# Turning the combined attention weights in 32-square pieces on VectorE and through DRAM, for chunks 3 to 11 of a sliding-window attention and feed-forward kernel

## The chip, the cores and the metric

The kernel runs on 1 core of one Trainium2 chip. The metric is the device time of one execution in microseconds (us). The kernel before takes 695.46 us (median of 3 runs, 695.16 to 696.05).

## The reference

Attention over 4 batches, 8 heads, 768 positions and head size 64, where a query sees only the 4 first keys (sinks) and the last 128 keys. The output, 3072 tokens by 512, goes through two matrix products with a leaky rectifier between them. All of it is float32.

```python
scores = scale * q @ k.T                     # per batch and head, 768 x 768
keep = (key < n_sink) | ((query - key >= 0) & (query - key < window))
a = softmax(where(keep, scores, -1e9))
x = (a @ v) laid out as (3072, 512)
h = x @ w_in                                 # (3072, 2048)
g = maximum(h, 0) + alpha * minimum(h, 0)
out = g @ w_out                              # (3072, 512)
```

## The kernel before, in words

**Tiling.** The 3072 tokens are cut into 12 chunks of 256 queries (`NCHUNK`), three to a batch. A chunk is two query tiles of 128 (`u` is 0 or 1). For a head of a chunk there are three blocks of 128 keys and the 4 sinks. The heads are taken in four pairs (`p` is 0 to 3, `j` the head within its pair).

**Attention of a chunk** (`attention(c)`, in steps). Head by head: `prep_head` splits queries and keys of a loaded tile `stage` into high and low parts (L553 to L557); `unit` makes the scores by two matmuls into a bank `s` (L589, L590); `soften` adds the mask and takes the row's extreme on VectorE (L602), then the exponential on ScalarE (L606). `finish_head` takes the sums' reciprocals (L635, L636). Of a query tile's two key blocks, the older one is used only above the diagonal and the newer one only below and on it, so that both fit in one 128 by 128 square. L647 (L643 for the first tile of a batch) adds them, scaled, into the tile `comb`: 128 queries by 512, which holds four such squares, (head of the pair, query tile). `comb` tiles come from a ring of 4. After the eighth head `sink_step` prepares the sinks (L674, L675, L680, L683).

**Turning the weights.** The product with the values needs the weights with keys on the partitions. `trans(c, p)` does it for chunks 2 to 11: four TensorE transposes per pair, one per square, into one PSUM bank (L694), then two VectorE products of 512 elements each (L698) that read the bank, multiply by two triangles of ones (`tri`) and so part the older from the newer block again, into a tile `wa` (ring of 2). Chunks 0 and 1 (`SPLIT`) do this in another way and do not call it. From chunk 3 on (`PAIRED`) the steps at the end are: `trans` of pairs 0 and 1, `av_two(c, 0)`, `trans` of pairs 2 and 3, `av_two(c, 2)`. `av_two` multiplies two pairs with the sinks (L781) and the values (L711, in 24 or 16 short matmuls), and splits the result into `xh` and `xl` (L791, L792).

**Feed-forward of a chunk.** Sixteen slots `f`. `gemm1` (L806): 12 matmuls of 256 columns into one of two banks `h`; ScalarE and VectorE turn it into `gh` and `gl` (L810 to L813); `gemm2`, two slots later (`LAG`): six matmuls of 512 columns (L843, L844, L841). While chunk c is in its feed-forward, the steps of chunk c+1's attention are spread over its slots 1 to 12 (`SPAN`); slots 13 to 15 have none. The first `gemm1` of a chunk needs all of `xh` and `xl`.

**The order of the work** is computed by the class `Plan`. Each operation is recorded with its engine, a cost, and what it reads and writes. `draw` then runs a clock for each engine and picks, at each step, an operation that can begin soonest; among those of one engine that can begin within a short time it takes the one of lowest rank. The rank of a TensorE operation is its place in the program; any other operation has that of the first TensorE operation that needs it. A DMA issue on SP costs 0.45 us in the plan, and its data counts as landed 2 us, and the time for its bytes at 290 GB/s, after it begins. Every engine then gets its instructions in the planned order and works through them in that order, waiting where the planned time was wrong. Buffers of one ring (a "kind") are handed out strictly in the order in which the program asked for them:

```python
if len(f) <= n or not any(q[x] is v for x in range(min(len(q), n + 1))):
    ok = False
```

So a later `comb` tile can't be given out in the plan while an earlier request of that ring is still unserved. SP's queue carries the loads of `stage` (ring of 2, L436), the values (L451) and the stores of the output (L850).

Of the kernel before, what the change touches and what calls it, by code (L numbers as in the profile page):

```python
# [9 lines left out]
F32 = mybir.dt.float32  # L10
# [7 lines left out]
ALU = mybir.AluOpType  # L18

P = 128  # L20
# [23 lines left out]
PAIRED = 3  # L44
# [34 lines left out]
class Plan:  # L79
# [20 lines left out]
    def held(self, tile_):  # L100
        v = Value(None)
        v.at = tile_
        return v

    def op(self, engine, cost, run, reads=(), writes=(), tail=0.09, mode=None, nbytes=0, other=None, locks=False):
        o = Op(engine, cost, tail, run, self.rank if engine == "PE" else None)
        o.ways = {engine: (cost, run)}
        if other:
            o.ways[other[0]] = other[1:]
        o.born = self.rank  # L110
        if engine == "PE":
            self.rank += 1
        o.mode, o.nbytes, o.index = mode, nbytes, len(self.ops)
        seen = []
        for group, writing in ((reads, False), (writes, True)):
            for x in group:
                v, key = x if isinstance(x, tuple) else (x, None)
                if v not in seen:
                    seen.append(v)
                keys = [k for k in set(v.wrote) | set(v.read) if key is None or k is None or k == key]  # L120
                for k in keys:
                    o.before.update(v.wrote.get(k, ()))
                    if writing:
                        o.before.update(v.read.get(k, ()))
                if writing:
                    for k in keys:
                        if key is None or k == key:
                            v.wrote.pop(k, None)
                            v.read.pop(k, None)
                    v.wrote.setdefault(key, []).append(o)  # L130
                else:
                    v.read.setdefault(key, []).append(o)
        for v in seen:
            v.left += 1
        o.values = seen
        o.takes = [v for v in seen if v.kind]
        o.locks = locks
        self.ops.append(o)
        return o
# [144 lines left out]
def dve(n, fast=False):  # L284
    return 0.07 + (0.52e-3 if fast else 1.04e-3) * n


def cast(n, psum=False):
    return (0.045 if psum else 0.092) + 0.84e-3 * n
# [27 lines left out]
ISSUE = 0.45  # L317
# [3 lines left out]
def program(ctx, tc, qk, pairs, vp, vs, w, par, out):  # L321
    nc = tc.nc
# [4 lines left out]
    plan = Plan(tc)  # L327
    op, val, held = plan.op, plan.value, plan.held
# [5 lines left out]
    def several(name, n, shape, dtype):  # L334
        plan.kind(name, [pool.tile(shape, dtype, name=f"{name}{i}") for i in range(n)])

    several("stage", 2, [P, QC + KC], F32)
    several("kq", 2, [P, KC + 2 * QC], F32R)
    several("v", 2, [P, 3, 2, D], F32)
# [131 lines left out]
    def known(x):  # L471
        return V.setdefault(x, held(x))
# [38 lines left out]
    tri = pool.tile([P, 2, P], F32, name="tri")  # L511
# [27 lines left out]
    xh, xl, prep, comb, sink, ptile_, sums, rinv, nms, wt = {}, {}, {}, {}, {}, {}, {}, {}, {}, {}  # L539

    def bank(c, n, tag):
        return val("o" if c == 0 and n % 2 else tag)
# [67 lines left out]
    def finish_head(c, h):  # L610
        pt, nm, sm = ptile_.pop((c, h)), nms[c], sums[c]
        sk = sink[c]
        if h == H - 1:
            op("DVE", 0.1, lambda: nc.vector.tensor_tensor(fm, fm, nm.at.rearrange("p h u -> p (h u)"), ALU.max),
               reads=[nm], writes=[known("fm")])
        if c in SPLIT:
            op("POOL", 0.17, lambda: nc.gpsimd.tensor_copy(sk.at[:, :, h], pt.at[:, :, P:P + NS]), reads=[pt], writes=[(sk, h)])
            tp = bank(c, h, "pa")
            for u in range(2):
                o = 2 * u * P  # L620
                both = u > 0 or c % CPB > 0

                def turn(u=u, o=o, both=both):
                    if both:
                        nc.tensor.transpose(tp.at[:, o:o + P], pt.at[:, u, 0:P], ident)
                    nc.tensor.transpose(tp.at[:, o + P:o + 2 * P], pt.at[:, u, P + NS:], ident)
                op("PE", (1 + both) * TURN, turn, reads=[(pt, u), known("ident")], writes=[tp], tail=T_TAIL)
            t = val("comb")
            o = P if c % CPB == 0 else 0
            op("ACT", cast(4 * P - o, True), lambda: nc.scalar.copy(t.at[:, o:], tp.at[:, o:]), reads=[tp], writes=[t],  # L630
               other=("DVE", dve(4 * P - o), lambda: nc.vector.tensor_copy(t.at[:, o:], tp.at[:, o:])) if c == 0 else None)
            wt.setdefault((c, h // 2), []).append(t)
            return
        ri = val("ri")
        op("DVE", 0.15, lambda: nc.vector.tensor_scalar(ri.at[:, :2], sm.at[:, h], 1e-9, None, op0=ALU.add), reads=[(sm, (h, 0)), (sm, (h, 1))], writes=[ri])  # L635
        op("DVE", 0.08, lambda: nc.vector.reciprocal(ri.at[:, :2], ri.at[:, :2]), writes=[ri])  # L636
        if h % 2 == 0:
            comb[c, h // 2] = val("comb")
        cb = comb[c, h // 2]
        view = lambda: cb.at.rearrange("p (j u x) -> p j u x", j=2, u=2)[:, h % 2]  # L640
        for u in range(2):
            if u == 0 and c % CPB == 0:
                op("DVE", 0.2, lambda: nc.vector.tensor_scalar(view()[:, 0], pt.at[:, 0, P + NS:], ri.at[:, 0:1], None, op0=ALU.mult),  # L643
                   reads=[(pt, 0), ri], writes=[(cb, (h % 2, 0))])
                continue
            jk = val("jk")
            op("DVE", 0.28, lambda u=u, jk=jk: nc.vector.tensor_tensor_reduce(  # L647
                out=view()[:, u], in0=pt.at[:, u, 0:P], in1=pt.at[:, u, P + NS:], scale=ri.at[:, u:u + 1], scalar=0.0,
                op0=ALU.add, op1=ALU.max, accum_out=jk.at[:, u:u + 1]),
                reads=[(pt, u), ri], writes=[(cb, (h % 2, u)), jk])  # L650
        op("POOL", 0.2, lambda: nc.gpsimd.tensor_tensor(
            sk.at[:, :, h], pt.at[:, :, P:P + NS], ri.at[:, :2].unsqueeze(2).broadcast_to([P, 2, NS]), ALU.mult),
            reads=[pt, ri], writes=[(sk, h)])

    sinkT = {}

# [28 lines left out]
    def trans(c, p):  # L685
        if c in SPLIT:
            return
        tp, cb, tt = val("pa"), comb.pop((c, p)), val("wa")
        full = lambda: tt.at.bitcast(F32).rearrange("p (j u l x) -> p j u l x", j=2, u=2, l=2)

        def turn(j):
            for u in range(2):
                o = (2 * j + u) * P
                nc.tensor.transpose(tp.at[:, o:o + P], cb.at[:, o:o + P], ident)  # L694
        for j in range(2):
            op("PE", 2 * TURN, lambda j=j: turn(j), reads=[(cb, (j, 0)), (cb, (j, 1))], writes=[(tp, j)], tail=T_TAIL)
        for j in range(2):
            op("DVE", dve(4 * P), lambda j=j: nc.vector.tensor_tensor(  # L698
                full()[:, j], tp.at[:, j * QC:(j + 1) * QC].rearrange("p (u x) -> p u x", u=2).unsqueeze(2).broadcast_to([P, 2, 2, P]),
                tri.unsqueeze(1).broadcast_to([P, 2, 2, P]), ALU.mult), reads=[(tp, j), known("tri")], writes=[(tt, j)])  # L700
        wt[c, p] = tt

    def values(c, v, weights, a, stop=True):

        sets = [(1, slice(P, 3 * P), slice(0, 2 * P))]
        if c % CPB:
            sets.append((0, slice(0, P), slice(0, P)))
        sets.append((2, slice(3 * P, 4 * P), slice(P, 2 * P)))
        for n, (blk, ws, os) in enumerate(sets):
            for j in range(2):  # L710
                nc.tensor.matmul(a[j * D:(j + 1) * D, os], v[:, blk, j], weights(j)[:, ws], start=False, stop=stop and n == len(sets) - 1)  # L711
# [149 lines left out]
    def attention(c):  # L861
        def a_step(h, u):
            def run():
                if u == 0:
                    if h == 0 and c and c % CPB == 0:
                        vs_prep(c // CPB)
                    prep_head(c, h)
                    next_load()
                unit(c, h, u)
                if u == 1:  # L870
                    finish_head(c, h)
                    if h in (5, 6):
                        load_v(c, h - 5)
            return run
# [139 lines left out]
    with tc.If(bad != 0):  # L1014
# [3 lines left out]
        with tc.For_i(0, B, 1) as b:  # L1018
            for cc in range(CPB):
                x = general(nc, gen, ptile, cc, b, qk5, vp5, nsink, window, ident)  # L1020
# [162 lines left out]
```

## Time and profile before

| | |
|---|---|
| median of 3 runs | 695.46 us |
| the profiled execution: time, span | 695.24 us, 693.3 us |
| busy TensorE, VectorE, ScalarE, GpSimd | 680.6, 497.2, 408.2, 32.2 us |
| L694: TensorE transposes | 160, mean 273 ns from start to end |
| L698: VectorE products out of the bank | 80, mean 685 ns |
| DMA | 63.71 MB, 28155 packets |

The page of the profile gives busy times by engine, the span in 40 slices, the DMA queues, and the chain of work that ended last. Views of the trace give groups of instructions by line, stretches of time (windows), the chain in order of time, and the timeline of one engine. Matmuls overlap, so the mean time of one from start to end is longer than what it adds to the chain; VectorE's instructions overlap slightly too, so its "slot" is the distance from one start to the next.

### The profile page before, as it was taken

How to read it: one execution, taken by the hardware profiler on the slowest of the kernel's cores; microseconds unless marked ns; L12 is line 12 of the kernel's file. 1: busy time of each engine (PE TensorE's matmuls, PEld its weight loads, DVE VectorE, ACT ScalarE, POOL GpSimd, SP SyncE). 2: the span in 40 equal slices, each digit the busy share in tenths (PEclk: the TensorE clock that was granted, in tenths of full speed). 3: DMA queues.
4: the chain of work that ended last, by engine and by line, in shares of the span. 5: the costliest groups of instructions: out<-in, count | busy, mean ns of one | idle time of the engine just before them, and what ended most of it. 6: DMA issues, size and time to landing. Idle time of an engine off the chain costs nothing.

```text
span 693.3 us, 13330 instructions
## 1 busy us (share of the span) xinstructions
PE 680.6 (98%) x4694; PEld 598.1 (86%) x4696; DVE 497.2 (72%) x1651; ACT 408.2 (59%) x1093; POOL 32.2 (5%) x115
## 2 busy tenths in 40 slices
PE   9989999999999999999999999999999999999996
PEld 4568898879889989989989989988988988998985
DVE  6999999968748847946965965974883984884231
ACT  6989977647538527636736725834743852842332
POOL 2110000000000000000000000000000000000000
PEclk9999999999999999999999999999999999999999
DMA  8765542332203213222222222311320421300001
GB/s 317 271 225 182 179 160 61 122 113 83 77 24 110 76 47 117 65 65 88 60 85 70 78 80 71 98 62 54 116 62 24 135 65 33 109 0 25 30 2 35
DMA packets 28155, 63.71 MB, mean 92 GB/s; under 512 B 2992, under 2 KB 9136, under 8 KB 28080
## 3 DMA queue, kind: packets, MB, share of 16 engines
q1 hardware_dynamic: 24528, 49.66, 22.6%
q10 hardware_dynamic: 3552, 13.11, 5.4%
q8 instruction: 39, 0.64, 0.4%
q14 instruction: 36, 0.29, 0.1%
HBM read 56.47 MB, written 6.29 MB: 91 GB/s over the span
## 4 chain that ended last, share of the span: by engine, by line
PE 86%; DVE 9%; ACT 3%; issue 1%; POOL 0%; DMA 0%; ACTq 0%; DVEq 0%
PE bank L806 35%; PE bank L841 12%; PE bank L843 12%; PE bank L844 11%; PE bank L711 5%; PE bank L589 3%; PE bank L590 3%; PE bank L694 3%; DVE wa L391 2%; DVE w L399 1%; ACT pt L606 1%; DVE wa L389 1%; ACT wa L377 1%; DVE gl L813 1%; DVE g L811 1%
## 5 line engine op out<-in xcount | busy, mean ns | idle before, releaser
L806 PE MATMUL bank<-xh,w 128*128 128x256 f32 x1536 | 314.2, 283 | 1.4 <-DVE g L811 1.2
L806 PEld LDWEIGHTS bank<-xh,w 128*128 128x128 f32 x1536 | 252.7, 189 | 9.2 <-DVE g L811 2.0
L806 PE MATMUL bank<-xl,w 128*128 128x256 f32 x768 | 214.6, 279 | 0.0
L810 ACT ACTIVATE g<-bank,param 128x256 f32<-128x256 f32 x192 | 90.4, 472 | 142.2 <-PE bank L806 140.0
L843 PE MATMUL bank<-w,gh 128*128 128x512 f32 x382 | 152.4, 399 | 0.0
L844 PE MATMUL bank<-w,gh 128*128 128x512 f32 x382 | 149.9, 392 | 0.0
L806 PEld LDWEIGHTS bank<-xl,w 128*128 128x128 f32 x768 | 145.1, 189 | 5.2
L811 DVE TENSOR_TENSOR g<-bank,g 128x256 f32<-128x256 f32 x192 | 80.4, 420 | 88.6 <-ACT g L810 87.8
L841 PE MATMUL bank<-w,gl 128*128 128x512 f32 x382 | 120.5, 397 | 0.0
L812 ACT CAST gh<-g 128x256 fp32r<-128x256 f32 x192 | 77.3, 404 | 71.0 <-DVE g L811 70.0
L606 ACT ACTIVATE pt<-pt,nm 128x260 f32<-128x260 f32 (+1 forms) x192 | 94.2, 491 | 24.5 <-DVE nm L602 23.9
L813 DVE TENSOR_TENSOR gl<-g,gh 128x256 fp32r<-128x256 f32 x192 | 81.0, 423 | 37.6 <-ACT gh L812 35.9
L602 DVE CUSTOM_DVE_ANT_0 pt<-bank,masks 128x260 f32<-128x260 f32 (+1 forms) x192 | 75.0, 402 | 15.2 <-PE bank L590 11.9
L841 PEld LDWEIGHTS bank<-w,gl 128*128 128x128 f32 x382 | 69.3, 188 | 15.4 <-issue 2.1
L843 PEld LDWEIGHTS bank<-w,gh 128*128 128x128 f32 x382 | 71.8, 188 | 8.4 <-ACT kq L553 0.2
L844 PEld LDWEIGHTS bank<-w,gh 128*128 128x128 f32 x382 | 71.9, 188 | 8.3
L698 DVE TENSOR_TENSOR wa<-bank,tri 128x512 f32<-128x512 f32 x80 | 50.7, 685 | 14.2 <-PE bank L694 14.1
L555 DVE TENSOR_TENSOR kq<-stage,kq 64x392 fp32r<-64x392 f32 x80 | 45.2, 566 | 10.1 <-ACT kq L553 8.1
L553 ACT CAST kq<-stage 128x392 fp32r<-128x392 f32 x80 | 41.5, 519 | 8.9 <-PE bank L590 6.2
L590 PE MATMUL bank<-kq 128*128 128x260 f32 (+1 forms) x160 | 44.3, 281 | 0.0
L647 DVE CUSTOM_DVE_ANT_0 comb<-pt,ri 128x128 f32<-128x128 f32 x136 | 44.1, 347 | 0.0
L589 PE MATMUL bank<-kq 128*128 128x260 f32 (+1 forms) x160 | 43.8, 278 | 0.1
(123 smaller groups left out, 665.6 us busy)
## 6 DMA issues: line engine op xcount, KB each, us to landing
stage<-qk SPq DMA_DIRECT2D x80, 324.0 KB, 2.8
wraw<-w ACTq DMA_DIRECT2D x12, 1024.0 KB, 5.2
v<-vp SPq DMA_DIRECT2D x44, 192.0 KB, 2.5
out_dram<-ob SPq DMA_DIRECT2D x22, 256.0 KB, 2.2
wraw<-w SPq DMA_DIRECT2D x4, 1024.0 KB, 12.2
lent<-pairs SPq DMA_DIRECT2D x4, 324.0 KB, 3.8
stage<-pairs SPq DMA_DIRECT2D x4, 324.0 KB, 8.0
ob<-vs SPq DMA_DIRECT2D x4, 256.0 KB, 3.1
```

The lines of the kernel that those rows point to most:

```text
L589: nc.tensor.matmul(s[:, w0], qh()[:, qs], ks()[:, kw], start=True, stop=False)
L590: nc.tensor.matmul(s[:, w0], ql()[:, qs], ks()[:, kw], start=False, stop=True)
L602: op("DVE", dve(n), lambda: nc.vector.tensor_tensor_reduce(out=pt.at[:, u, w0], in0=s.at[:, w0], in1=masks[:, i, w0], scale=-0.125, scalar ...
L606: op("ACT", exp(n), lambda: nc.scalar.activation(pt.at[:, u, w0], pt.at[:, u, w0], AF.Exp, bias=nm.at[:, h, u:u + 1], scale=-1.0, accum_ou ...
L806: nc.tensor.matmul(h(), fin.at[:, 0, part, ks], rhs.at[:, kt], start=(kt == 0 and n == 0), stop=(kt == KT - 1 and n == 2))
L810: op("ACT", act(QC, True), lambda: nc.scalar.activation(g.at, h(), AF.Copy, scale=alt[:, f:f + 1]), reads=[bk, known("param")], writes=[g])
L811: op("DVE", dve(QC), lambda: nc.vector.tensor_tensor(g.at, h(), g.at, ALU.max), reads=[bk], writes=[g])
L812: op("ACT", cast(QC), lambda: nc.scalar.copy(gh.at, g.at), reads=[g], writes=[gh])
L813: op("DVE", dve(QC), lambda: nc.vector.tensor_tensor(gl.at, g.at, gh.at.bitcast(F32), ALU.subtract), reads=[g, gh], writes=[gl])
L841: nc.tensor.matmul(o2[j].at, gl.at[:, js], fin.at[:, 1, 0], start=False, stop=(f == NF - 1))
L843: nc.tensor.matmul(o2[j].at, gh.at[:, js], fin.at[:, 1, 0], start=(f == 0), stop=False)
L844: nc.tensor.matmul(o2[j].at, gh.at[:, js], fin.at[:, 1, 1], start=False, stop=False)
```

## The change

For chunks 3 to 11 `trans` no longer uses TensorE. As soon as a pair's second head is finished, `swap(c, p)` does three things. VectorE turns the 512 columns of `comb` in squares of 32 by 32, each in its own place, into a second tile of the same ring (`small`), with the pieces sorted by the group of 32 partitions to which they must go. SP stores this tile to DRAM (256 KB, 512 bytes a row). SP then loads it back by four DMAs of 64 KB, each into 32 partitions of a third tile of the ring (`t`). `swapped(c, p)`, at the place where `trans` stood, multiplies by the triangles, now out of SBUF and in four VectorE products of 256 elements each. The ring of `comb` keeps its 4 tiles and `wa` its 2. There are two tiles in DRAM. Chunk 2 stays as it was.

```diff
@@ program
+    scratch = ctx.enter_context(tc.tile_pool(name="scratch", bufs=1, space=bass.MemoryType.DRAM))
+    plan.kind("swap", [scratch.tile([4, P, P], F32, name=f"swap{i}") for i in range(2)])
     several("stage", 2, [P, QC + KC], F32)
@@ finish_head
             reads=[pt, ri], writes=[(sk, h)])
+        if c >= PAIRED and h % 2:
+            swap(c, h // 2)
@@ trans
         if c in SPLIT:
             return
+        if c >= PAIRED:
+            return swapped(c, p)
         tp, cb, tt = val("pa"), comb.pop((c, p)), val("wa")
@@ after trans
+    def swap(c, p):
+
+        cb = comb.pop((c, p))
+        small, d, t = val("comb"), val("swap"), val("comb")
+        op("DVE", dve(4 * P), lambda: nc.vector.transpose(
+            small.at.rearrange("p (j t b) -> p t j b", t=4, j=4), cb.at.rearrange("p (t j b) -> p t j b", t=4, j=4)),
+            reads=[(cb, (j, u)) for j in range(2) for u in range(2)], writes=[small])
+        op("SP", ISSUE, lambda: nc.sync.dma_start(d.at.rearrange("j p x -> p j x"), small.at.rearrange("p (j x) -> p j x", j=4)),
+           reads=[small], writes=[d], nbytes=4 * P * 4 * P)
+        for j in range(4):
+            op("SP", ISSUE, lambda j=j: nc.sync.dma_start(
+                t.at[j * 32:(j + 1) * 32].rearrange("a (i x) -> a i x", i=4), d.at[j].rearrange("(i a) x -> a i x", i=4)),
+               reads=[d], writes=[(t, j)], nbytes=4 * P * P)
+        turned[c, p] = t
+
+    def swapped(c, p):
+        t, tt = turned.pop((c, p)), val("wa")
+        full = lambda: tt.at.bitcast(F32).rearrange("p (j u l x) -> p j u l x", j=2, u=2, l=2)
+        view = lambda: t.at.rearrange("p (i j u b) -> p j u i b", i=4, j=2, u=2)
+        for j in range(2):
+            for u in range(2):
+                op("DVE", dve(2 * P), lambda j=j, u=u: nc.vector.tensor_tensor(
+                    full()[:, j, u].rearrange("p l (i b) -> p l i b", i=4),
+                    view()[:, j, u].unsqueeze(1).broadcast_to([P, 2, 4, 32]),
+                    tri.rearrange("p l (i b) -> p l i b", i=4), ALU.mult), reads=[t, known("tri")], writes=[(tt, (j, u))])
+        wt[c, p] = tt
+
+    turned = {}
```

## The prediction, made before the result was known

> **What bounds the kernel now.** I read the page first (busy times, the clock, the chain), then windows, then the chain in order of time.
>
> ```profile
> span 693.3 us, 13330 instructions
> ...
> PE 680.6 (98%) x4694; PEld 598.1 (86%) x4696; DVE 497.2 (72%) x1651; ACT 408.2 (59%) x1093; POOL 32.2 (5%) x115
> ...
> PEclk9999999999999999999999999999999999999999
> ...
> PE 86%; DVE 9%; ACT 3%; issue 1%; POOL 0%; DMA 0%; ACTq 0%; DVEq 0%
> PE bank L806 35%; PE bank L841 12%; PE bank L843 12%; PE bank L844 11%; PE bank L711 5%; PE bank L589 3%; PE bank L590 3%; PE bank L694 3%; DVE wa L391 2%; DVE w L399 1%; ACT pt L606 1%; DVE wa L389 1%; ACT wa L377 1%; DVE gl L813 1%; DVE g L811 1%
> ```
>
> The chain runs through TensorE for 86% of the span, and the transposes (L694) are 3% of it. A busy share of 98% doesn't yet say that TensorE is never kept waiting where the change acts, so I asked for windows. The first two below are whole chunks; the last two are the two halves of one chunk's attention, its heads and its turning and products. Columns: length, then busy time of TensorE, weight loads, VectorE, ScalarE and GpSimd, the clock, the DMA share, GB/s.
>
> ```profile
> 187.00:241.00 54.00, 54.00 (x377) 48.69 (x375) 38.99 (x144) 30.70 (x87) 1.69 (x8) 1.00 0.24 74
> 568.50:623.00 54.50, 54.50 (x390) 49.32 (x386) 37.55 (x142) 29.05 (x83) 2.11 (x8) 1.00 0.16 50
> ```
> ```profile
> 592.00:620.00 28.00, 28.00 (x190) 25.73 (x189) 25.59 (x113) 20.08 (x62) 2.11 (x8) 1.00 0.22 68
> 620.00:636.00 16.00, 16.00 (x133) 13.95 (x132) 8.00 (x17) 4.25 (x11) 0.00 (x0) 1.00 0.09 26
> ```
>
> TensorE is busy for all 54.00 us of a chunk at the full clock, so here each matmul taken off it shortens the time, as long as nothing keeps it waiting instead. VectorE is not idle beside it: 25.59 of 28.00 us in the heads phase, and 8.00 of 16.00 after it. So the gain lies on TensorE, the danger on VectorE and on the new trip through DRAM.
>
> **TensorE: what goes.** The chain in order of time gives the price of the transposes in place.
>
> ```profile
> 619.82 0.46 PE bank L841 x2
> 620.28 0.44 PE bank L694 x4
> 620.71 1.39 PE bank L806 x12
> ...
> 630.76 1.89 PE bank L711 x24
> ...
> 640.12 1.39 PE bank L806 x12
> ```
> ```profile
> L694 PE MATMUL bank<-ident,comb 128*128 128x128 f32 x160 | 24.0, 273 | 0.0
> L698 DVE TENSOR_TENSOR wa<-bank,tri 128x512 f32<-128x512 f32 x80 | 50.7, 685 | 14.2 <-PE bank L694 14.1
> L813 DVE TENSOR_TENSOR gl<-g,gh 128x256 fp32r<-128x256 f32 x192 | 81.0, 423 | 37.6 <-ACT gh L812 35.9 <-PE bank L958 0.5
> L391 DVE SCALAR_TENSOR_TENSOR wa<-wraw,wa 128x1024 int32<-128x1024 int32 x16 | 19.5, 1217 | 0.1
> L381 DVE TENSOR_SCALAR wa<-wa 128x1024 int32<-128x1024 int32 x8 | 5.5, 686 | 0.3 <-ACT wa L377 0.3
> ```
>
> The four transposes of a pair add 0.44 us to the chain, and the L806 group behind them takes its usual 1.39. So a transpose costs TensorE 0.11 us, though it lasts 273 ns from start to end: the next matmul starts before it ends. Nine chunks of four pairs make 36 x 0.44 = 15.84 us. The Trainium skill, "TensorE: Matmul & The Clock Gate" (Part 4: PE-mode transpose), gives some 275 ns for a transpose in a kernel, which the 273 ns here confirm; the 144 that go would by that figure be worth 39 us, an estimate which the 0.44 us for four rules out.
>
> **VectorE: what it loses and gains.** Its timeline gives the slots, which are shorter than the durations.
>
> ```profile
> 609.34 0.35 DVE L647 CUSTOM_DVE_ANT_0 comb<-pt,ri 128x128 f32<-128x128 f32 x1
> 609.61 0.35 DVE L647 CUSTOM_DVE_ANT_0 comb<-pt,ri 128x128 f32<-128x128 f32 x1
> ...
> 612.77 0.35 DVE L647 CUSTOM_DVE_ANT_0 comb<-pt,ri 128x128 f32<-128x128 f32 x1
> ...
> 613.40 0.34 DVE L647 CUSTOM_DVE_ANT_0 comb<-pt,ri 128x128 f32<-128x128 f32 x1
> ...
> 616.90 0.34 DVE L647 CUSTOM_DVE_ANT_0 comb<-pt,ri 128x128 f32<-128x128 f32 x1
> ...
> 620.75 1.29 DVE L698 TENSOR_TENSOR wa<-bank,tri 128x512 f32<-128x512 f32 x2
> ...
> 634.15 0.75 DVE L792 TENSOR_TENSOR xl<-bank,xh 128x256 fp32r<-128x256 f32 x2
> ```
>
> Two products of 512 take 1.29 us, 0.645 each; 72 of them go, 46.4 us. Two of 256 take 0.75 with a last one of 0.42, so that a slot of 256 is 0.33; 144 come, 47.5 us. The 32-square turning of 512 columns isn't in the trace. Its lower bound is half the fast 1024-element L381, 0.34 us; its upper one, if each element took two passes, is L391's 1.22 for 1024. I take 0.645, as L698 handles as many elements at one a step; 36 make 23.2 us. The sum for VectorE is +24.3 us, 2.7 a chunk (1.6 to 5.0 by the bounds). The Trainium skill, "VectorE: DVE Perf Modes" (The three transpose paths), has 311 ns for a bf16 square of 128, so four would take 1.24 us, an estimate at the upper bound; no run here shows it yet.
>
> A whole chunk has room for that: 38.99 + 2.7 = 41.7 of some 52.2 us. The heads phase hasn't: four turnings (2.6 us) and perhaps the products of pairs 0 and 1 (2.6), which no longer wait for the end, against 2.4 us idle. So the heads phase gets up to some 3 us longer. The 8 us idle after it takes that up, since the products of pairs 0 and 1 leave it.
>
> **The trip through DRAM.** This is the added wait.
>
> ```profile
> stage<-qk SPq DMA_DIRECT2D x80, 324.0 KB, 2.8
> ...
> v<-vp SPq DMA_DIRECT2D x44, 192.0 KB, 2.5
> out_dram<-ob SPq DMA_DIRECT2D x22, 256.0 KB, 2.2
> ...
> param<-par SPq DMA_DIRECT2D x1, 10.0 KB, 1.8
> ```
> ```profile
> L451 SPq DMA_DIRECT2D v<-vp x44: 327/328/862, 11.6 to 625.2; - x44
> ```
>
> A store of the same 256 KB lands after 2.2 us. The new one has rows of 512 bytes, a quarter of `ob`'s, so I allow 2.2 to 4 and take 2.7. The loads of 64 KB lie between param's 1.8 and v's 2.5 us; four issues at 0.33 (L451) put the last one 1.0 later, so 3.2 us. With the turning, one trip is 0.65 + 2.7 + 3.2, about 6.5 us. The plan's own formula gives about as much: 2.9 for the store, then 1.35 for three issues and 2.2 for the last load. So the planned places of the waits should fit.
>
> Who is queued behind it? On SP each set of loads waits for its store, and `stage` loads planned later stand behind. A `stage` tile is wanted again two heads after it comes free, some 6 us as the heads phase goes (28 us for eight heads, 3.5 each); its load takes 2.8, so 3 us of standing is covered. On VectorE the multiplications wait for the loads, with L811 and L813 of the feed-forward behind them. And there is the ring of `comb`: requests are served in order, so the first L647 of the next pair can't be placed before the first load of this pair is issued. That is 0.27 (one L647 slot) + 0.65 + 2.7 + some 0.2 for the hops, 3.8 us from a pair's last L647. In the rows above, the next pair's first L647 comes 0.27 us (609.34 to 609.61) and 0.63 us (612.77 to 613.40) after it; now they would be near 613.1 and, behind pair 2's own, 617.8. The last L647 moves from 616.90 to about 619, with the fuller VectorE to 620 or 621. Add 6.5 us and four products of 0.33, and pair 3's weights are ready near 628. The values of pairs 2 and 3 (L711) started at 630.76, so nothing is late yet. Behind it stands a second reserve, which needs one more row.
>
> ```profile
> 645.64 1.07 ACT L849 COPY ob<-bank 128x512 f32<-128x512 f32 x2
> ```
>
> L849 reads out the sum of chunk 10 when its last matmul is done, at 645.64; two `gemm1` and two `gemm2` of 1.38 us each lie before that, so chunk 11's first `gemm1` is the one at 640.12. Its last input (L792 x2) was there at 634.15 + 0.75 = 634.90: 5.2 us early. Taking 1.76 us of transposes (4 x 0.44) out of each chunk brings that `gemm1` forward, so the reserve is 2.8 + 5.2 - 1.8, about 6 us in all.
>
> **The sum.** 695.24 (span 693.3 and 1.94 around it) less 15.84 is 679.4. I add 1.5 us, about 0.2 a chunk, for short standing of TensorE behind a fuller VectorE: 680.9, and as the profiled execution lies 0.2 below the median, 681.0.
>
> **The rivals.** *The turning comes late, a little.* If VectorE's turning costs the upper bound and, being of low rank, waits a microsecond or two in the heads phase, the attention of a chunk is 7 us later instead of 6 at most: 1 us of TensorE's time lost in each of nine chunks, 681 + 9, about 690 (684 to 694). For it speaks VectorE's 25.59 of 28.00; against it the 8 us idle behind.
>
> *No change.* The same at 1.6 us a chunk more than is covered: 695.
>
> *The trip is longer than the plan holds it for.* Two of the pairs' gaps and the last trip lie one behind the other, so x us more per trip is 3x per chunk. Beyond the 6 us of reserve TensorE stands at the chunk's first `gemm1`; the gain is used up at 3x = 6 + 1.8, so x = 2.6, a trip of 9 us. At x = 3 it loses 9 - 6 = 3 us in each of nine chunks: 695.2 - 15.8 + 27, about 706. For it: four times as many rows in the store as in `ob`, each trip a store and a load in series, and an engine that works in order behind them. Against it: the DMA share is 0.16 to 0.24. The Trainium skill's "VectorE: DVE Perf Modes" (Rules for kernel authors) would leave a 128 by 128 transpose to TensorE where PSUM will do as the target, and VectorE's transpose for squares of 32 alone. It speaks for this rival; but TensorE is the engine with nothing to spare in this trace, and no run here shows yet which way it falls.
>
> *A larger gain* would need TensorE to wait for the transposes now; the windows show no such wait, so 15.84 is the ceiling.
>
> **How the numbers follow.** Forecast 0.54 (its own range 678.5 to 684), a partial gain 0.18, no change 0.07, the long trip 0.21. Faster by over 0.2% (1.4 us, about what a measurement of this kernel can tell) is 0.54 + 0.18 = 0.72; same 0.07; slower 0.21. The range starts at 678.5, the ceiling with a margin under it of 0.9, and reaches 700, into the milder half of the long trip, so that some 2 in 10 are left out.
>
> **What would show it.** Right: L694 falls to 16, TensorE's windows from chunk 3 on stay full, a chunk is 1.76 us shorter, VectorE's busy time rises by about 24 us to some 521, the store lands in 2.2 to 4 us and a trip is about 6.5. The partial gain would show as idle time of L806's weight loads behind L792 at the start of a chunk. The long trip would show as VectorE idle until a DMA into `comb`, and L811 late in the same stretch. I am wrong if TensorE stands though a trip is below 9 us, or if the four products of 256 or the turning are much longer than 0.33 and 0.65.

## The result and the profile after

The changed kernel takes 680.12 us (median of 4 runs, 679.48 to 681.45) against 695.75 us for the kernel before (4 runs beside it): a ratio of 0.9778, with a 95% interval of 0.976 to 0.9795. The forecast was 681.0.

The page of the changed kernel's profile, the lines that answer to those of before. Its lines have moved: `gemm1` is now L841, its VectorE steps L846 and L848, `gemm2` L876 to L879, the values L746, the combined weights L649.

```profile
span 678.4 us, 13475 instructions
...
PE 665.8 (98%) x4552; PEld 582.2 (86%) x4552; DVE 522.7 (77%) x1759; ACT 407.2 (60%) x1093; POOL 31.7 (5%) x115
...
q1 hardware_dynamic: 64272, 68.55, 34.1%
```

TensorE has 142 instructions fewer in the record and is still busy for 98% of a span that is 14.9 us shorter. VectorE has 25.5 us more (497.2 before). The groups by line show the new work, and what is left of the old: the 16 transposes of chunk 2.

```profile
L713 DVE STREAM_TRANSPOSE comb<-comb 128x512 f32<-128x512 f32 x36 | 25.3, 703 | 0.4
L730 DVE TENSOR_TENSOR wa<-comb,tri 128x256 f32<-128x256 f32 x144 | 52.4, 419 | 12.4 <-DMA comb<-swap 12.2
...
L700 PE MATMUL bank<-ident,comb 128*128 128x128 f32 x16 | 2.5, 275 | 0.0
```

The DMA issues, with KB each and the median from issue to landing:

```profile
swap<-comb SPq DMA_DIRECT2D x36, 256.0 KB, 2.2
comb<-swap SPq DMA_DIRECT2D x144, 64.0 KB, 2.1
```

Whole chunk, then the heads phase and what follows it in the attention of chunk 11 (length, busy time of TensorE, weight loads, VectorE, ScalarE, GpSimd):

```profile
187.00:241.00 54.00, 54.00 (x372) 48.41 (x370) 42.36 (x153) 30.92 (x89) 1.65 (x8) 1.00 0.40 115
```
```profile
579.00:607.00 28.00, 28.00 (x190) 25.61 (x189) 25.97 (x108) 20.15 (x61) 2.08 (x8) 1.00 0.36 105
607.00:623.00 16.00, 16.00 (x117) 14.00 (x116) 11.01 (x36) 5.01 (x13) 0.00 (x0) 1.00 0.33 92
```

TensorE is as full as before; VectorE's new work lies for the most part in the second stretch (11.01 us where it had 8.00). A chunk's own length is read from ScalarE's copies of its finished sum, three chunks in a row, of before and after:

```profile
372.54 1.06 ACT L849 COPY ob<-bank 128x512 f32<-128x512 f32 x2
427.44 1.07 ACT L849 COPY ob<-bank 128x512 f32<-128x512 f32 x2
482.14 1.07 ACT L849 COPY ob<-bank 128x512 f32<-128x512 f32 x2
```
```profile
366.41 1.06 ACT L884 COPY ob<-bank 128x512 f32<-128x512 f32 x2
419.47 1.07 ACT L884 COPY ob<-bank 128x512 f32<-128x512 f32 x2
472.31 1.07 ACT L884 COPY ob<-bank 128x512 f32<-128x512 f32 x2
```

The two chunks lasted 54.90 and 54.70 us and now last 53.06 and 52.84, 1.84 and 1.86 less; four groups of transposes were 1.76. Over the eight chunks from the copy at 208.97 to that at 645.64 before, and from 207.94 to 631.01 after, it is 13.60 us, 1.70 a chunk (1.46 to 1.86).

### The profile page after: what moved, and what is told of

It is laid out like the page before. It is cut to its first block, busy times and chain, and to the rows that moved or that the text cites. A ratio compares the mean times of both kernels' runs of the same rounds, so it can differ in the third digit from the quotient of the medians.

```text
span 678.4 us, 13475 instructions
## 1 busy us (share of the span) xinstructions
PE 665.8 (98%) x4552; PEld 582.2 (86%) x4552; DVE 522.7 (77%) x1759; ACT 407.2 (60%) x1093; POOL 31.7 (5%) x115
## 3 DMA queue, kind: packets, MB, share of 16 engines
q1 hardware_dynamic: 64272, 68.55, 34.1%
## 4 chain that ended last, share of the span: by engine, by line
PE 82%; DVE 9%; ACT 5%; issue 1%; DMA 1%; POOL 0%; SPq 0%; ACTq 0%; DVEq 0%
PE bank L841 34%; PE bank L878 12%; PE bank L876 11%; PE bank L879 11%; PE bank L746 5%; PE bank L591 3%; PE bank L592 3%; DVE wa L393 2%; DVE w L401 2%; ACT pt L608 1%; ACT wa L379 1%; DVE wa L391 1%; DVE gl L848 1%; PE bank L1031 1%; DVE g L846 1%
## 5 line engine op out<-in xcount | busy, mean ns | idle before, releaser
L841 PE MATMUL bank<-xh,w 128*128 128x256 f32 x1536 | 307.7, 281 | 1.7 <-DVE g L846 1.5
L841 PEld LDWEIGHTS bank<-xh,w 128*128 128x128 f32 x1536 | 251.0, 189 | 10.6 <-DVE g L846 3.4
L841 PE MATMUL bank<-xl,w 128*128 128x256 f32 x768 | 214.8, 280 | 0.0
L879 PE MATMUL bank<-w,gh 128*128 128x512 f32 x382 | 149.9, 392 | 0.0
L841 PEld LDWEIGHTS bank<-xl,w 128*128 128x128 f32 x768 | 145.2, 189 | 5.3
L846 DVE TENSOR_TENSOR g<-bank,g 128x256 f32<-128x256 f32 x192 | 80.1, 419 | 58.2 <-ACT g L845 57.4
L876 PE MATMUL bank<-w,gl 128*128 128x512 f32 x382 | 119.9, 395 | 0.0
L847 ACT CAST gh<-g 128x256 fp32r<-128x256 f32 x192 | 77.1, 404 | 66.8 <-DVE g L846 65.8
L608 ACT ACTIVATE pt<-pt,nm 128x260 f32<-128x260 f32 (+1 forms) x192 | 94.0, 490 | 17.7 <-DVE nm L604 17.1
L848 DVE TENSOR_TENSOR gl<-g,gh 128x256 fp32r<-128x256 f32 x192 | 81.1, 424 | 30.2 <-ACT gh L847 27.6
L876 PEld LDWEIGHTS bank<-w,gl 128*128 128x128 f32 x382 | 69.7, 188 | 14.5 <-issue 0.7
L604 DVE CUSTOM_DVE_ANT_0 pt<-bank,masks 128x260 f32<-128x260 f32 (+1 forms) x192 | 73.9, 400 | 8.5 <-PE bank L592 5.5
L879 PEld LDWEIGHTS bank<-w,gh 128*128 128x128 f32 x382 | 71.9, 188 | 8.3
L730 DVE TENSOR_TENSOR wa<-comb,tri 128x256 f32<-128x256 f32 x144 | 52.4, 419 | 12.4 <-DMA comb<-swap 12.2
L557 DVE TENSOR_TENSOR kq<-stage,kq 64x392 fp32r<-64x392 f32 x80 | 45.3, 566 | 10.7 <-ACT kq L555 8.7
L555 ACT CAST kq<-stage 128x392 fp32r<-128x392 f32 x80 | 41.5, 519 | 10.6 <-PE bank L592 7.3
L592 PE MATMUL bank<-kq 128*128 128x260 f32 (+1 forms) x160 | 44.5, 281 | 0.0
L591 PE MATMUL bank<-kq 128*128 128x260 f32 (+1 forms) x160 | 44.0, 279 | 0.1
L649 DVE CUSTOM_DVE_ANT_0 comb<-pt,ri 128x128 f32<-128x128 f32 x136 | 43.1, 346 | 0.0
```

The costliest lines, as they stand in the source:

```text
L591: nc.tensor.matmul(s[:, w0], qh()[:, qs], ks()[:, kw], start=True, stop=False)
L592: nc.tensor.matmul(s[:, w0], ql()[:, qs], ks()[:, kw], start=False, stop=True)
L604: op("DVE", dve(n), lambda: nc.vector.tensor_tensor_reduce(out=pt.at[:, u, w0], in0=s.at[:, w0], in1=masks[:, i, w0], scale=-0.125, scalar ...
L608: op("ACT", exp(n), lambda: nc.scalar.activation(pt.at[:, u, w0], pt.at[:, u, w0], AF.Exp, bias=nm.at[:, h, u:u + 1], scale=-1.0, accum_ou ...
L841: nc.tensor.matmul(h(), fin.at[:, 0, part, ks], rhs.at[:, kt], start=(kt == 0 and n == 0), stop=(kt == KT - 1 and n == 2))
L846: op("DVE", dve(QC), lambda: nc.vector.tensor_tensor(g.at, h(), g.at, ALU.max), reads=[bk], writes=[g])
```

## The experiments

Two theories stood at first. **Freed slots**: the gain is TensorE's time in the transposes, and everything added is hidden. **Relief**: it comes from waits that went with them. Later ones ask how well the added work is hidden. Each run has the changed kernel as its base, and its ratio is to the kernel before.

**1. Dead transposes put back (e1_pe_back).**

```diff
         if c >= PAIRED:
+            tp = val("pa")
...
+                    nc.tensor.transpose(tp.at[:, o:o + P], ident, ident)
             return swapped(c, p)
```

> The changed kernel, with four TensorE transposes per pair put back where they stood in chunks 3 to 11, but of the constant unit square and with a result that nothing reads; the turn on VectorE and the trip through DRAM stay. Theory of the freed slots (the gain is the TensorE time of the transposes, all else is hidden): 680.1 + 36 x 0.44 = 696, the time of before within 1 us, and TensorE full in each chunk. Rival, relief (the gain comes from VectorE no longer waiting for the transposes, 14.1 us before, and from the banks they held): the dead transposes are waited for by nobody, so the time stays below 688.

Measured: 695.41 us, ratio 1.0003 (0.9994 to 1.0013). Transposes whose result nobody reads take the whole gain away, while the turn and the trip are still there. The gain is TensorE's slots; relief of VectorE falls. The PSUM banks are taken again too, so this run alone doesn't part slots from banks; but the kernel before had TensorE busy for all 54.00 us of a chunk, so it didn't wait for a bank there. Run 1 also shows that turn and trip cost nothing that can be measured beside a TensorE with the old amount of work.

**2. No turn and no trip (e2_no_trip).**

```diff
-        small, d, t = val("comb"), val("swap"), val("comb")
...
+        t = cb
```

> The changed kernel without turn, store and loads: the products with the triangles read the combined weights as they are, so the weights of chunks 3 to 11 stay unturned and the output is not the reference's. TensorE's work is that of the changed kernel. Freed slots, all else hidden: the same as the changed kernel within 1 us, 679 to 680.5. Rival, a paid remainder (the trip and VectorE's 25 us cost a few us that the gain hides): 675 to 678.

Measured: 679.18 us, 0.9765 (0.9751 to 0.9778). The interval overlaps that of the changed kernel. All that is still paid for turn and trip is 0.9 us by the medians, or nothing.

**3. The turn made twice (e3_turn_twice).**

```diff
         op("DVE", dve(4 * P), lambda: nc.vector.transpose(
...
+        op("DVE", dve(4 * P), lambda: nc.vector.transpose(
...
```

> VectorE's turn of a pair made twice, 36 x 0.70 = 25 us more on VectorE, in the heads phase. Freed slots: VectorE still has room, within 1.5 us of the changed kernel, 680 to 681.5. Rival, thin reserve (a chunk's attention has 2 to 3 us left before TensorE must wait for it): two turns lie behind each other before a pair's loads, 4 x 0.7 = 2.8 us later per chunk, of which up to 1 us is paid in nine chunks: 684 to 690.

Measured: 687.40 us, 0.9877 (0.9859 to 0.9895), 7.3 us more than the changed kernel. So the cover is thin somewhere. VectorE's timeline shows more than 0.7 us of delay: the second turn (L716) waits behind other work, 3.7 us after the first or 0.9.

```profile
437.63 0.69 DVE L713 STREAM_TRANSPOSE comb<-comb 128x512 f32<-128x512 f32 x1
...
441.30 0.69 DVE L716 STREAM_TRANSPOSE comb<-comb 128x512 f32<-128x512 f32 x1
...
447.04 0.70 DVE L713 STREAM_TRANSPOSE comb<-comb 128x512 f32<-128x512 f32 x1
...
447.91 0.69 DVE L716 STREAM_TRANSPOSE comb<-comb 128x512 f32<-128x512 f32 x1
```

**4. One more DMA in each trip (e4_hop).**

```diff
+        e = val("hop")
+        op("SP", ISSUE, lambda d=d: nc.sync.dma_start(e.at.rearrange("j p x -> (j p) x"), d.at.rearrange("j p x -> (j p) x")),
+           reads=[d], writes=[e], nbytes=4 * P * 4 * P)
...
```

The four loads then read this copy.

> One more DMA in each trip: the stored 256 KB are copied within DRAM before they are loaded, some 2.6 us more per trip (a store lands after 2.2 us in the trace, with 0.4 for its issue). Reserve as predicted, 6 us a chunk and three trips in series: 7.8 - 6 = 1.8 us lost in nine chunks, 696. Thin reserve, 2 to 3 us as the trace of the changed kernel shows for chunk 11: 7.8 - 3 = 4.8 in nine chunks, 723. Rival, only the last trip counts (the others lie beside the heads): 2.6 us more is just covered, 680 to 683.

Measured: 692.76 us, 0.9967 (0.9953 to 0.9982), 12.6 us more than the changed kernel. The copy takes longer than a store, and VectorE now stands for the loads twice as long (columns of the second view: us in total, times, longest; the changed kernel had 12.2, 12 and 2.6).

```profile
hop<-swap SPq DMA_DIRECT2D x36, 256.0 KB, 3.0
```
```profile
DVE wa L734 <- DMA comb<-hop: 23.8, 19, 2.8
...
PE bank L592 <- DVE nm L605: 3.3, 7, 0.7
```

The time is nearest to the 696 of the predicted reserve; the reserve read from one chunk's trace would have made it 723. A trip of some 10 us instead of 6.6 takes four fifths of the gain. TensorE is busy 5.7 us more than in the changed kernel (671.5 against 665.8) and stands 6.7 us more; its waits in the view (L592 for the masked scores of L605, here 3.3 us) do not add up to the 12.6 us. So I don't take the match of 3x minus 6 for a proof of that formula.

**5. Turn, store and loads ranked first (e5_turn_first).** As the trace shows a turn starting late in VectorE's queue, I gave these operations the rank of the place where they are asked for.

```diff
+        for o in plan.ops[n:]:
+            o.rank = plan.rank
```

> The changed kernel, with turn, store and loads ranked at the place in the program where they are asked for, and so ahead of VectorE's work for later steps. In the trace of the changed kernel a turn starts 1.4 to 3.8 us after its pair's last L649; this should fall below 1 us, and chunk 11's last inputs, ready at 626.2 us, should come 2 us earlier or more. As TensorE doesn't stand in the changed kernel, the time stays within 1.5 us of it, 679 to 681 (freed slots). If the turns were paid somewhere after all, 677 to 678.5.

Measured: 709.45 us, 1.0205 (1.0191 to 1.0219): 29 us slower than the changed kernel, where no change was expected. TensorE's longest waits in all: `gemm1` (L843 here) stands for VectorE's L848, which reads its bank out, and the scores (L591) stand for ScalarE's L555, which itself stands for the loads of `stage`.

```profile
ACT kq L555 <- DMA stage<-qk: 13.5, 10, 2.0
...
PE bank L843 <- DVE g L848: 12.0, 19, 0.9
...
PE bank L591 <- ACT kq L555: 5.4, 4, 1.4
```

Two things may be behind this. In `link` an operation has the rank of the earliest that needs it. A turn of early rank hands it back to L649, L608 and L604, and the whole softmax goes ahead of the feed-forward on VectorE. And the stores and loads of the trip, ranked early too, go ahead of the loads of `stage` on SP; in the changed kernel the same view shows no wait for `stage`.

**6. The same with the added DMA (e6_hop_turn_first).** Both edits, 4 and 5.

```diff
+        e = val("hop")
...
+        for o in plan.ops[n:]:
+            o.rank = plan.rank
```

> The kernel with one more DMA in each trip (692.8 us), with the ranks of the run before. If the low rank of the turns used up the reserve, the lost 12.6 us come back for the most part: 680 to 685. If the trip itself is too long for the ring of the combined weights, whatever the rank: 689 to 693.

Measured: 701.50 us, 1.0085 (1.007 to 1.0101). Outside both expectations: worse than run 4, which has no such ranks, and 8 us better than run 5, which has no added DMA; the latter stays unexplained. As the loss of run 5 is in it, it says nothing on the ring.

**7. From chunk 2 on (e7_chunk2).** The condition in `finish_head` and in `trans`.

```diff
-        if c >= PAIRED and h % 2:
+        if c >= PAIRED - 1 and h % 2:
...
-        if c >= PAIRED:
+        if c >= PAIRED - 1:
```

> The change extended to chunk 2, so that no chunk from 2 on is turned by TensorE: 16 transposes fewer, 4 x 0.44 = 1.76 us by freed slots, 678.4, if chunk 2's attention, which ends while weights are still being converted on VectorE up to some 105 us, has room; 680 to 682 if it hasn't.

Measured: 680.43 us, 0.9791 (0.9778 to 0.9805): no gain over the changed kernel. The stretch 134 to 160 us, in which chunk 2 is turned, first in the changed kernel, then in this one:

```profile
134.00:160.00 26.00, 25.34 (x184) 21.18 (x184) 18.90 (x56) 13.11 (x38) 1.69 (x3) 1.00 0.37 106
```
```profile
134.00:160.00 26.00, 24.02 (x165) 19.03 (x165) 22.38 (x83) 14.50 (x43) 2.03 (x3) 1.00 0.54 154
```

TensorE was nearly full there (25.34 of 26 us) and is now busy 1.3 us less, so most of the freed 1.76 us became idle time. VectorE has 3.5 us more to do in the stretch; what TensorE waits for was not followed.

**8. Load beside the trip (e8_load_beside).** Two turns of 256 columns of a constant per pair, which nobody waits for.

```diff
+        for n in range(2):
+            op("DVE", dve(2 * P), lambda: nc.vector.transpose(
+                geof.rearrange("p a w -> p (a w)")[:, :2 * P], tri.rearrange("p l x -> p (l x)")),
...
```

> As with the doubled turn, some 25 us more on VectorE (two turns of 256 columns per pair, of a constant into a tile that nothing reads), but beside the trip, so that no load waits for them. If the doubled turn's 7.3 us came from the later loads: 680 to 682. If they came from VectorE's load in the heads phase: 685 to 689.

Measured: 704.47 us, 1.014 (1.0124 to 1.0155), outside both expectations, and the edit didn't do what it was meant to. The turns needed nothing but a constant, so the plan began them as soon as VectorE had gaps, and the timeline has them up to 140 us, ahead of chunk 2's softmax. TensorE then stood, and its clock fell (the last three columns are the clock, the DMA share and GB/s). From 187 to 640 us TensorE is busy for all 453 us, as in the changed kernel, so the loss lies in this early stretch, and the run doesn't tell what such a load costs in the heads phase.

```profile
135.00:140.00 5.00, 5.00 (x29) 4.15 (x27) 4.83 (x14) 1.29 (x3) 0.00 (x0) 1.00 0.00 0
140.00:145.00 5.00, 2.38 (x10) 1.19 (x8) 4.58 (x22) 3.94 (x12) 0.26 (x1) 0.99 0.20 40
145.00:150.00 5.00, 2.81 (x8) 1.94 (x8) 4.31 (x22) 3.75 (x13) 0.40 (x2) 0.50 0.59 159
```

**9. The turn's rank alone (e9_turn_only_first).** Set after `link`, so that nothing inherits it.

```diff
+        first.append(op("DVE", dve(4 * P), lambda: nc.vector.transpose(
...
     plan.link()
+    for o in first:
+        o.rank = o.born
```

> As the run that ranked turn, store and loads first, but the rank of the 36 turns alone is changed, after the other ranks are set, so that the softmax steps ahead of a turn don't inherit it. Theory of the inherited rank (those 29 us came from L604 to L649 being planned ahead of the feed-forward's L846 and L848, for which TensorE then stood): the loss is gone, 679 to 681, and turns start below 1 us after their pair's last L649. Rival, the early turn itself is what harms: above 700.

Measured: 679.94 us, 0.9773 (0.9753 to 0.9792), as the changed kernel. So the early turn itself costs nothing, and the 29 us of run 5 came from what else was raised there: the inherited rank, or the stores and loads on SP, which keep their rank here. The two were not tried apart. The turn now starts at once, here for a first pair: the last L649 at 431.11, the turn 0.39 us later, where the changed kernel had 1.93.

```profile
431.11 0.35 DVE L649 CUSTOM_DVE_ANT_0 comb<-pt,ri 128x128 f32<-128x128 f32 x1
...
431.50 0.71 DVE L713 STREAM_TRANSPOSE comb<-comb 128x512 f32<-128x512 f32 x1
```
```profile
431.36 0.35 DVE L649 CUSTOM_DVE_ANT_0 comb<-pt,ri 128x128 f32<-128x128 f32 x1
...
433.29 0.69 DVE L713 STREAM_TRANSPOSE comb<-comb 128x512 f32<-128x512 f32 x1
```

That a trip ends earlier brings nothing, as TensorE isn't waiting for it.

**10. The load in the gaps (e10_load_in_gaps).** Run 8 mended: each dead turn is planned behind its pair's real one and has the lowest rank.

```diff
...
+            o.rank = o.born + 400
+            plan.order_after(o, turn)
```

> The 25 us of added VectorE work beside the trip once more, but each pair's two turns of a constant are planned behind the pair's own turn and at the lowest rank, so that they fill gaps. If VectorE's load as such isn't the limit, but only where it lies: 680 to 682, with VectorE some 25 us busier than in the changed kernel. If any 25 us more on VectorE cost time: 685 to 689, as with the doubled turn.

Measured: 679.73 us, 0.9757 (0.9739 to 0.9776), as the changed kernel, with VectorE at 546.5 us.

```profile
PE 665.1 (98%) x4550; PEld 582.5 (86%) x4552; DVE 546.5 (81%) x1831; ACT 406.3 (60%) x1093; POOL 31.1 (5%) x115
```

The doubled turn (run 3) kept VectorE busy for 545.3 us and cost 7.3 us. The same load costs nothing where it may wait and nobody waits for it.

**11. The added DMA with the turn's rank alone (e11_hop_turn_only_first).** Edits 4 and 9.

```diff
+        e = val("hop")
...
+    for o in first:
+        o.rank = o.born
```

> The kernel with one more DMA in each trip (692.8 us), with the rank of the turns alone raised. If the turns' late start used up the reserve of a chunk, some 2 us of each of the trips in series come back: 681 to 687. If a trip of some 10 us is too long for the ring of the combined weights whatever the turn's place: 690 to 693.

Measured: 690.81 us, 0.9917 (0.9897 to 0.9938). 2.0 us less than run 4 by the medians (3.5 by the ratios), within the 690 to 693 expected for a trip too long: the late start of the turns is a small part of what the longer trip costs.

**12. The doubled turn, both ranked first (e12_turn_twice_first).**

```diff
-        op("DVE", dve(4 * P), lambda: nc.vector.transpose(
+        for n in range(2):
+            first.append(op("DVE", dve(4 * P), lambda: nc.vector.transpose(
...
+    for o in first:
+        o.rank = o.born
```

> The doubled turn once more, with the ranks of both turns alone raised, so that the second stands right behind the first. In the trace of the doubled turn the second started 0.9 to 3.7 us after the first, behind other work of VectorE. If that queueing, added to each trip, took its 7.3 us: 680 to 682, since 0.7 us more per trip is less than what the early turn gains. If two turns in the trip cost time by their length: 685 to 688.

Measured: 687.97 us, 0.99 (0.9886 to 0.9914), as run 3. My reading of run 3 falls: the second turn's queueing wasn't the price. TensorE's waits, and VectorE's timeline in one chunk:

```profile
PE bank L842 <- DVE g L847: 5.4, 10, 0.7
```
```profile
447.87 0.41 DVE L847 TENSOR_TENSOR g<-bank,g 128x256 f32<-128x256 f32 x1
...
450.44 1.46 DVE L714 STREAM_TRANSPOSE comb<-comb 128x512 f32<-128x512 f32 x2
...
453.15 1.09 DVE L731 TENSOR_TENSOR wa<-comb,tri 128x256 f32<-128x256 f32 x3
454.15 0.75 DVE L847 TENSOR_TENSOR g<-bank,g 128x256 f32<-128x256 f32 x2
```

Here the feed-forward's L847 comes 6.3 us after the last one (454.15 less 447.87), then twice in a row, behind the turns and the products of the weights; `gemm1` (L842) stands for it. So in this run time is lost in the middle of a chunk and not by `xh` and `xl` coming late, for which the waits have a single one of 0.3 us. The wait for L847 was 1.5 us in the changed kernel, so it accounts for 3.9 of the 7.3 us by which the span is longer (685.7 against 678.4); TensorE's busy time is 2.9 longer, and why is open. Why the plan packs VectorE so, by its cost of 0.60 us for a turn of 0.70 or otherwise, was not tried.

## Why the prediction was right, point by point

- **The sum.** 36 groups at 0.44 us, 15.84, less 1.5. Measured by the medians 15.63, and run 1 shows that it is this term. The allowance was too large: some 0.9 us is paid, or nothing (run 2). Two slips of arithmetic change nothing: 680.9 and 0.2 make 681.1, and VectorE's lower bound is 1.5 us a chunk, not 1.6.
- **VectorE.** +24.3 us forecast, +25.5 measured. The products have 419 ns and were sized by a slot of 0.33; the turn lasts 703 ns for 512 columns, near the one-pass value of 0.645 that I took, and far from the upper bound. The Trainium skill, "VectorE: DVE Perf Modes" (The three transpose paths), has 311 ns for a 128 by 128 bf16 turn; four such squares in one float32 instruction took 703 ns here, 176 each, so the estimate of 1.24 us from that figure was too high.
- **The trip.** 2.7 for the store and 3.2 for the loads were forecast. The store lands after 2.2 although it has four times the rows of `ob`'s. The loads land after 2.1, but their issues are slower than the 0.33 us of L451. The first pair's trip in chunk 11's attention, SP's queue and VectorE's:

```profile
594.84 1.75 SPq L719 DMA_DIRECT2D comb<-swap x4
```
```profile
589.75 0.35 DVE L649 CUSTOM_DVE_ANT_0 comb<-pt,ri 128x128 f32<-128x128 f32 x1
...
591.68 0.69 DVE L713 STREAM_TRANSPOSE comb<-comb 128x512 f32<-128x512 f32 x1
...
595.32 0.33 DVE L649 CUSTOM_DVE_ANT_0 comb<-pt,ri 128x128 f32<-128x128 f32 x1
...
603.77 0.35 DVE L649 CUSTOM_DVE_ANT_0 comb<-pt,ri 128x128 f32<-128x128 f32 x1
...
607.70 0.70 DVE L713 STREAM_TRANSPOSE comb<-comb 128x512 f32<-128x512 f32 x1
...
611.08 0.34 DVE L649 CUSTOM_DVE_ANT_0 comb<-pt,ri 128x128 f32<-128x128 f32 x1
...
611.89 0.35 DVE L649 CUSTOM_DVE_ANT_0 comb<-pt,ri 128x128 f32<-128x128 f32 x1
...
625.82 0.42 DVE L827 TENSOR_TENSOR xl<-bank,xh 128x256 fp32r<-128x256 f32 x1 [0.45 <-ACT xh L826]
```

  Four issues take 1.75 us, so the last is some 1.3 after 594.84 and lands near 598.3: 6.6 us from the start of the turn, forecast 6.5. The last pair's trip is longer, about 8.2 us by the same reckoning (turn at 612.28, loads issued from 617.05 on): its store is issued at 614.11, behind a load of values on SP.
- **The ring of `comb`: the step that was off.** Forecast was 3.8 us from a pair's last L649 to the next pair's first. It is 5.6 for the first pair (589.75 to 595.32), since the turn itself waits in VectorE's queue, 1.9 us here, and 7.3 for the third (603.77 to 611.08), whose turn waits 3.9. I had put that wait only into a rival. The last L649 is at 611.89, 19.1 us ahead of the copy of chunk 10's sum, which L884 makes at 631.01; before it was 28.7 us ahead (616.90 and 645.64). That is 9.6 us nearer, where the forecast (620 or 621 for the 616.90, and 1.8 for the shorter chunk) gave 5 to 6. Chunk 11's last input, at 625.82 + 0.42 = 626.24, is there 4.8 us ahead of the copy, where it was 10.7 (634.90). The first `gemm1` stood 5.5 us ahead of the copy. So of the reserve, which I put at about 6 us after the change, nothing is left in this reckoning: the input is 0.7 us late.
- **Why it still cost nothing.** The reckoning takes the first `gemm1` of a chunk for one piece that needs all of `xh` and `xl`. In the kernel it is four parts of three matmuls, one for each pair of heads, and a part needs only its pair's `xh` and `xl`. TensorE's chain, and then ScalarE's queue and one weight load of TensorE:

```profile
623.13 0.35 PE bank L841 x3
623.48 1.89 PE bank L746 x24
625.37 0.55 PE bank L841 x3
...
627.32 2.06 PE bank L841 x18
629.38 0.23 PE bank L878
```
```profile
629.42 0.41 ACT L847 CAST gh<-g 128x256 fp32r<-128x256 f32 x1 [0.49 <-DVE g L846]
...
631.01 1.07 ACT L884 COPY ob<-bank 128x512 f32<-128x512 f32 x2
```
```profile
629.11 0.19 PEld L878 LDWEIGHTS bank<-w,gh 128*128 128x128 f32 x1
```

  The twelve matmuls 3, 3 and the first 6 of the 18 are one `gemm1`. Its result is cast (L847) only at 629.42, when the last `gemm2` before the copy has already loaded its weights `gh` (629.11); so that `gemm1` isn't chunk 10's but chunk 11's first. Its first six matmuls run before the last input is there, on the inputs of pairs 0 and 1 (ready at 614.55), and the six that need the rest begin at 627.32, 1.1 us after 626.24. The other twelve of the 18 are the second `gemm1`. So about 1 us is left in this chunk, not 6. The prediction has nothing of this division: that the time came out all the same in spite of the ring is luck. That TensorE would have stood without it is argued from these rows and was not tried.
- **The rivals.** A longer trip does cost time, but it was priced twice too dear: at 3 us more per trip 27 us were forecast, and run 4 with 3.0 us for the copy and its issue lost 12.6. So the gain isn't used up by 2.6 us more per trip. A partial gain came only with VectorE's turn doubled (runs 3 and 12), and in run 12 TensorE then stood in the middle of a chunk, not at the chunk's start. The rule of the Trainium skill, "VectorE: DVE Perf Modes" (Rules for kernel authors), to leave a 128 by 128 transpose to TensorE doesn't hold in this kernel: here TensorE is the engine without a gap, and taking 144 transposes off it made the kernel 2.2% faster.

## What to carry to other kernels

Where one engine is full in every window, price what you take off it by its step in the chain (0.11 us for a transpose), not by its duration (273 ns), and ask of everything you add only whether anything waits for it. Added work on another engine is free where it fills gaps and nobody waits for it, and dear where it is part of the trip, in a crowded phase: some 25 us more on VectorE cost nothing (run 10) or 7 us (run 3); which of the two counts, the place in the trip or the crowding, these runs don't part. In a list scheduler, check who inherits a priority that you raise, and what it overtakes in each queue: steps that feed the full engine must stay ahead of those with time to spare (run 5 lost 29 us, run 9 nothing).

## What the runs showed of the hardware

- A DMA of 512-byte rows wasn't slow for that: a store of 256 KB in such rows lands after 2.2 us like one of 2 KB rows. The added packets raise q1's share from 22.6% to 34.1% of 16 engines' span, (0.341 x 678.4 - 0.226 x 693.3) x 16 = 1194 us of one engine's time for the 39744 packets more on that queue (64272 less 24528), by this estimate 0.03 us for each.
- A copy of 256 KB within DRAM lands after 3.0 us, 0.8 more than the store.
- When TensorE was busy for only 2.38 of 5 us (run 8, 140 to 145 us), its granted clock was 0.50 in the next 5 us; a matmul of the scores (L592, 128x260) lasted 448 ns on average from 145 to 170 us, where it lasted 282 in the changed kernel, so the low clock added to the loss.
